# The held-back pair's products with v, moved behind the third bank of scores

## The chip, the cores and the metric

The kernel runs on one core of a Trainium2 chip. The metric is the device time of one execution in microseconds (us), taken over several runs. The core has five engines that run side by side, each through its own queue in order: TensorE (PE, matrix products; its weight loads are listed as PEld), VectorE (DVE), ScalarE (ACT), GpSimd (POOL) and SyncE (SP, which here only issues DMAs). They wait for each other through semaphores.

## The reference

Attention with a sliding window and a distance bias, for 8 batches of 8 heads, 576 positions and 64 channels, followed by a bilinear feed-forward layer on the joined heads:

```
scores = q @ k^T / sqrt(64) - slope[h] * |i - j|     masked to 0 <= i - j < 128
attn   = softmax(scores)          (max subtracted, 1e-9 added to the sum)
x      = attn @ v                 (heads side by side: 4608 tokens x 512)
out    = ((x @ w_a) * (x @ w_b)) @ w_out              (512 -> 1536 -> 512)
```

All inputs and the output are float32. q and k are scaled so that the scores spread over a wide range.

## The kernel before, in words

**Precision.** Nearly all products are done in float16 with each operand split into a high and a low part (high x high, high x low, low x high), accumulated in float32.

**Main work.** After the first batch, which has an order of its own, the program runs `batch(b)` for b = 1 to 7 (the second to the eighth batch). Each does the up products (`up`, 12 blocks of the hidden dimension) and then the down products (`down`). A block of the up products is done in one of two ways: plain (`up_plain`: four groups of twelve 128x128 by 128x288 matmuls, results in a ring of five PSUM banks) or fast (`up_fast`: seven groups of six, with fewer products and more additions). The second batch's blocks are all plain, the third's half and half, the fourth's two plain and ten fast, the later ones' all fast; the plain blocks come first. In the fast way two blocks are under way at once, each as a lane with its own `ch` bank that is written four times; between two writes ACT or DVE has to read it (L932, L944, L955, L967). These reads have a raised priority.

**Side work.** Under the main work of batch b runs the attention of batch b + 1 (`attention`, L710). It handles a batch as four pairs of heads, p = 0 to 3, and each pair in seven steps (the `yield i + k / 7`). For a pair: q and k are loaded, scaled and split (`squares`, `split_qk`, `low_qk`), laid out by SP's DMAs into `qst`, `qkh`, `qkl` (`lay_out_qk`), multiplied into scores in four banks (`scores`, L417: bank 0 holds three tiles, the others two), each followed by a minimum on DVE (L422) and an exponential on ACT (L423) into one of four `t` buffers. `normalize` writes the probabilities, split, into `phl`: the high half on ACT (L439), the low half on DVE (L440). `transpose_probs` (L445) is one transposing DMA from `phl` to `pT`, issued from SP. `pv` multiplies `pT` with the split v (`each_pv`, L541: 42 matmuls of 128x64 weights), and `keep_x` copies the result from PSUM on ACT (L454).

**The held-back pair.** There is one `phl` and one `pT`. Pair 0's probabilities are in `pT` while pair 1's are in `phl`. At p = 1 the products with v are skipped and pair 0 is put into `late`; they are done at p = 2, when v's scale for the batch is known. Only when they are done can pair 1's probabilities go from `phl` into `pT`, and only when that DMA is done may `normalize` of pair 2 write `phl`. `qtot` (L367) is a single small matmul in `split_qk` for the next pair.

**The order.** `Pace` ties the steps of the attention to the groups of the main work: a step is taken when the main work has passed its share. From batch 1 on PE's order is the order of the code (`manual_schedule` for PE). The order on ACT, DVE, POOL and SP is laid out ahead of time by a planner with a model of the run, by readiness and priority, and is then fixed. With `behind()`, an instruction is ordered behind the last main read on its engine. The pair p = 2 of batch b + 1 stands at the start of the up products of batch b: each of its steps takes a fourteenth of `up`, which in the fast way is six groups of six matmuls.

Buffers that matter: the score and product banks `at` are a ring of three (`ps_at`), used at p = 2 in the order scores 0, scores 1, vtot, then the two `x_ps`, qtot, scores 2, scores 3.

Of the kernel before, what the change touches and what calls it, by code (L numbers as in the profile page):

```python
# [46 lines left out]
def attention_then_bilinear_ffn(ctx: ExitStack, tc: tile.TileContext, qT, kT, vP, w_a, w_b, w_out, rel, slopes2, outT):  # L47
# [274 lines left out]
    def new_pT():  # L322
        return work.tile([P, 2 * NCOL // P, P], F16, tag="pT", name="pT")
# [52 lines left out]
    def low_qk(o, behind=None):  # L376
        with tc.issue_after(behind.ins) if behind else ExitStack():
            vec.scalar_tensor_tensor(out=o.kl.rearrange("p h s -> p (h s)"), in0=o.qk.rearrange("p h s -> p (h s)"), scalar=o.own, in1=o.kh.rearrange("p h s -> p (h s)"), op0=ALU.mult, op1=ALU.subtract)
# [23 lines left out]
    def scores(o, bi, ready=None):  # L402

        ps = ps_at.tile([P, 512], F32, tag="at", name="sc_ps")
        t = work.tile([P, 512], F32, tag="t", name="t", bufs=4)
        for i, c in BANKS[bi]:
            w = TILES[i][1]
            qq, kk = slice(64 * i, 64 * i + 64), slice(64 * i + 64 - w, 64 * i + 64)
            if o.b == 1:
                with tc.issue_after(last_pv[0].ins):  # L410
                    for e in range(2):
                        r = slice(64 * e, 64 * e + 64)
                        pe.matmul(ps[r, c:c + w], o.q[r, qq], o.k[r, kk], start=True, stop=True)  # L413
                continue
            for ks, last in ((o.kh, False), (o.kl, True)):
                for e in range(2):
                    pe.matmul(ps[64 * e:64 * e + 64, c:c + w], o.qs[:, e, qq], ks[:, e, kk], start=not last, stop=last)  # L417
        for i, c in BANKS[bi]:
            pc, w = TILES[i]
            n = o.n  # L420
            with tc.issue_after(ready.ins) if ready else ExitStack():
                beside[1] = vec.tensor_tensor_reduce(out=t[:, c:c + w], in0=ps[:, c:c + w], in1=o.bias[:, WIN - w:WIN], scale=-0.125 if o.b == 1 else o.neg, scalar=3.0e38, op0=ALU.add, op1=ALU.min, accum_out=o.mn[:, n:n + 1])  # L422
            beside[0] = act.activation(t[:, c:c + w], t[:, c:c + w], AF.Exp, bias=o.mn[:, n:n + 1], scale=-1.0, accum_out=o.sm[:, n:n + 1])  # L423
            o.parts.append((n, t[:, c:c + w], pc, w))
            o.n += 1
# [17 lines left out]
    def transpose_probs(o):  # L443
        o.pT = new_pT()
        sp.dma_start(o.pT, phl.rearrange("p a c -> p (a c)"), transpose=True)  # L445

    def new_x_ps():
        return [ps_at.tile([P, 512], F32, tag="at", name="x_ps") for _ in range(2)]

    def keep_x(p, st, xp, scale):  # L450

        x = st.v[:, p, 0:S]
        for ps, c, w in ((xp[0], 0, 512), (xp[1], 512, 64)):
            beside[0] = act.activation(x[:, c:c + w], ps[:, 0:w], AF.Copy, scale=scale)  # L454
        square_x(p, st, x)
# [74 lines left out]
    def each_pv(xp, vts, pts):  # L530

        for b in range(5):
            for rows, oc, blocks in by_keys(b):
                w = 64 * len(blocks)
                bank0, o0 = oc < 512, oc % 512
                first = oc == 0 if bank0 else b == 3
                ends = b == 3 if bank0 else b == 4
                for n, (vt, pt) in enumerate(zip(vts, pts)):
                    for h in range(2):
                        c = 512 + 64 * h if b == 4 else 64 * (4 * h + b)  # L540
                        last = pe.matmul(xp[oc // 512][64 * h:64 * h + 64, o0:o0 + w], vt[0:rows, c:c + 64], probs(pt, rows, blocks, h), start=(n == 0 and first), stop=(n == len(vts) - 1 and ends), skip_group_check=True)  # L541
        return last

    def pv(p, st, o, vhl):
        xp = new_x_ps()
        hi, lo = o.pT[:, 0:NCOL // P, :], o.pT[:, NCOL // P:2 * NCOL // P, :]
        each_pv(xp, (vhl[:, 0, :], vhl[:, 1, :], vhl[:, 0, :]), (hi, hi, lo))
        keep_x(p, st, xp, 1.0 / PSC)
# [161 lines left out]
    def attention():  # L710


        n = NPAIR * (B - 1)
        qks = {}

        def load(i):
            if i < n:

                qks[i] = (load_plain_qk if i < NPAIR else load_qk)(1 + i // NPAIR, i % NPAIR)

        def squares(i):
            if i >= n:
                return None
            qk = qks.pop(i)
            return qk if i < NPAIR else qk_squares(1 + i // NPAIR, i % NPAIR, qk)

        def split(o, whole=True):
            if o and o.b > 1:
                split_qk(o)
                if whole:  # L730
                    low_qk(o)

        def lay_out(o):
            if o:
                before_scores(o, lay_out_qk(o) if o.b > 1 else -8.0)

        def behind():

            return tc.issue_after(last_read[0].ins) if last_read[0] else ExitStack()

        load(0)
        st, prev = load_v(1), None
        o = squares(0)
        lay_out(o)
        load(1)
        yield 0
        for i in range(n + 1):
            b, p = 1 + i // NPAIR, i % NPAIR

            two = 2 if o and o.b >= 2 else 1  # L750
            if two == 2 and p == 1:
                with behind():
                    nxt = squares(i + 1)
            for bi in range(two if o else 0):
                scores(o, bi, nxt.ready if two == 2 and p == 1 and nxt else None)
            if two == 1 or p != 1:
                with behind():
                    nxt = squares(i + 1)
            if p == 1 and b > 1:
                st = load_v(b)  # L760
            if p == (1 if b == 1 else 2):
                v_scale(st)
            yield i + 1 / 7
            if o and two == 1:
                scores(o, 1)

            if p == 2:

                with tc.issue_after(first_reads[0].ins) if first_reads[0] else ExitStack():
                    late.vhl = split_v(st, late.p)  # L770
            elif prev and p != 1:
                prev.vhl = split_v(st, prev.p)
            yield i + 2 / 7
            if p == 2:
                pv(late.p, st, late, late.vhl)
                transpose_probs(prev)
                split(nxt)
            if o and p != 2:
                with behind():
                    normalize(o)  # L780
            if p != 2:
                split(nxt, p != 3)
            yield i + 3 / 7
            if o:
                scores(o, 2)
            if p == 3 and nxt and nxt.b > 1:
                low_qk(nxt, beside[1])
            if prev and p not in (1, 2):
                pv(prev.p, st, prev, prev.vhl)
            if two == 2 and p in (1, 3):  # L790
                if p == 2:
                    with behind():
                        normalize(o)
                scores(o, 3)
            yield i + 4 / 7
            if p == 2:
                prev.vhl = split_v(st, prev.p)
                if two == 1 or p not in (1, 3):
                    with behind():
                        normalize(o)  # L800
            if o and (two == 1 or p not in (1, 3)):
                scores(o, 3)
            lay_out(nxt)
            load(i + 2)
            if p == (0 if b == 1 else 1):
                v_squares(st, (0, 1))
            if prev and p == 0:
                states[b - 1] = st
                assert started["down"] == b - 2
                for k, _ in enumerate(split_x(st, b - 1 <= 3, b - 1 >= 2)):  # L810
                    yield i + (4.2 + 0.2 * k) / 7
            yield i + 5 / 7
            if o:
                with behind():
                    normalize(o)
            if p == (0 if b == 1 else 1):
                v_squares(st, (2, 3), vec if b > 2 else act)
            yield i + 6 / 7
            if prev and p == 0:
                hidden_scale(st)  # L820
            if p == 2:
                pv(prev.p, st, prev, prev.vhl)
            if p == 1:
                late = prev
            elif o:
                transpose_probs(o)
            prev, o = o, nxt
            yield i + 1
# [305 lines left out]
```

## Time and profile before

| what | value |
|---|---|
| median of 3 runs | 975.85 us (973.68 to 976.51) |
| the profiled execution | 975.07 us, of which its span 973.3 us |
| TensorE busy | 958.6 us, 98% of the span |
| VectorE, ScalarE busy | 683.1 us, 626.3 us |
| products of probabilities with v in float16 (L541) | 1176 matmuls, 42 for each of 28 pairs |
| transposing DMAs (L445) | 28, 6.9 us from issue to landing (median) |

How to read it: an engine's busy time counts its instructions, not its waits; the matmuls are pipelined, so that a listed length (286 ns for 128x288) is longer than the distance between two starts. In a timeline each line has the start in us from the span's start, the length, the engine, the line of the kernel, the operation, what it writes and reads, and a count where lines are merged; in brackets stands the idle time of that engine just before, with what ended it. "issue" means that nothing that the profile shows was waited for.

### The profile page before, as it was taken

The numbers are of one execution on the slowest core, as the hardware profiler recorded it, in microseconds if no ns is written. First come the engines' busy times: TensorE is split into PE (matmuls) and PEld (weight loads), VectorE is DVE, ScalarE is ACT, GpSimd is POOL, SyncE is SP. The second block draws the span as 40 slices with busy tenths as digits, with TensorE's granted clock in tenths as the row PEclk, the third lists the DMA queues.
The fourth block names the chain that finished last, engine by engine and source line by source line (L and its number), as shares of the span: only waits on it lengthen the run. The fifth ranks groups of instructions, "written<-read, shape, count | busy, mean of one in ns | idle before, by whom it ended". The sixth has DMA issues, their size and how long they took to land.

```text
span 973.3 us, 23844 instructions
## 1 busy us (share of the span) xinstructions
PE 958.6 (98%) x9340; PEld 747.8 (77%) x9341; DVE 683.1 (70%) x1896; ACT 626.3 (64%) x1701; POOL 260.7 (27%) x307
## 2 busy tenths in 40 slices
PE   8989999999999999999999999999999999999998
PEld 6667777777877777777877777777777778877776
DVE  6999998568888768887777877667676676514520
ACT  6878788577776666776766876767666765423321
POOL 1211122044546123631235222401222122301100
PEclk9999999999999999999999999999999999999999
DMA  9463736635347333464246552464245450210001
GB/s 351 143 259 111 254 84 135 146 102 111 90 97 171 75 69 72 109 158 93 52 92 172 101 104 50 111 177 93 45 94 130 117 100 12 57 37 2 1 13 37
DMA packets 148432, 102.82 MB, mean 106 GB/s; under 512 B 120032, under 2 KB 128352, under 8 KB 147296
## 3 DMA queue, kind: packets, MB, share of 16 engines
q1 hardware_dynamic: 138816, 91.77, 38.5%
q10 hardware_dynamic: 9504, 9.54, 3.1%
q8 instruction: 73, 1.20, 0.5%
q14 instruction: 39, 0.32, 0.1%
HBM read 48.33 MB, written 9.44 MB: 59 GB/s over the span
## 4 chain that ended last, share of the span: by engine, by line
PE 86%; DVE 5%; DMA 4%; ACT 3%; issue 1%; SPq 0%; POOL 0%; ACTq 0%; DVEq 0%
PE dn_ps L1003 23%; PE ch L907 19%; PE up_ps L907 17%; PE p L907 15%; PE x_ps L541 5%; PE sc_ps L417 4%; DMA v<-in_vP 2%; PE dn_ps L869 1%; PE sc_ps L413 1%; DMA pT<-phl 1%; DMA wdn<-in_w_b 1%; ACT vsq L309 1%; DVE phl L440 1%; DVE vsq L307 0%; DVE xs L476 0%
## 5 line engine op out<-in xcount | busy, mean ns | idle before, releaser
L907 PEld LDWEIGHTS <-wup 128*128 128x128 f16 x3072 | 296.5, 98 | 84.4 <-issue 7.9
L1003 PE MATMUL dn_ps<-h,wdn 128*128 128x288 f16 x2016 | 253.9, 286 | 0.0
L1003 PEld LDWEIGHTS <-wdn 128*128 128x128 f16 x2016 | 194.0, 98 | 51.8
L907 PE MATMUL up_ps<-xs,wup 128*128 128x288 f16 x1536 | 196.6, 287 | 2.8 <-DVE v L670 2.1
L962 POOL TENSOR_TENSOR rc<-rc,row 128x288 f32<-128x288 f32 x64 | 61.8, 966 | 275.1 <-DVE row L960 259.2
L907 PEld LDWEIGHTS <-wsum 128*128 128x128 f16 x1152 | 111.7, 98 | 30.9 <-issue 1.3
L423 ACT ACTIVATE t<-t,mn 128x192 f32<-128x192 f32 (+2 forms) x252 | 107.2, 427 | 26.4 <-DVE mn L422 26.2
L440 DVE SCALAR_TENSOR_TENSOR phl<-t,rin,phl 128x192 f16<-128x192 f32 (+2 forms) x252 | 107.1, 466 | 15.1 <-ACT phl L439 14.8
L907 PE MATMUL p<-xs,wup 128*128 128x288 f16 x768 | 115.0, 286 | 0.0
L907 PE MATMUL ch<-xs,wup 128*128 128x288 f16 x768 | 115.0, 286 | 0.0
L907 PE MATMUL ch<-xs,wsum 128*128 128x288 f16 x768 | 111.5, 286 | 0.4 <-ACT rc L932 0.4
L439 ACT ACTIVATE phl<-t,rin 128x192 f16<-128x192 f32 (+2 forms) x252 | 88.9, 425 | 29.2 <-DVE rin L436 15.6
L899 ACT CAST h<-rc 128x576 f16<-128x576 f32 x96 | 64.0, 668 | 63.1 <-DVE rc L967 38.1
L900 DVE TENSOR_TENSOR h<-rc,h 128x576 f16<-128x576 f32 x90 | 69.2, 770 | 29.8 <-ACT h L899 29.0
L422 DVE CUSTOM_DVE_ANT_0 t<-sc_ps,bias,neg 128x192 f32<-128x192 f32 (+2 forms) x216 | 73.6, 389 | 10.1 <-PE sc_ps L417 10.0
L1008 ACT ACTIVATE row<-dn_ps,oi 128x288 f32<-128x288 f32 x56 | 27.7, 494 | 57.3 <-PE dn_ps L1003 57.3
L476 DVE TENSOR_TENSOR xs<-v,xs 128x576 f16<-128x576 f32 x52 | 48.0, 934 | 22.5 <-ACT xs L475 22.4
L944 ACT ACTIVATE row<-ch,g 128x288 f32<-128x288 f32 x64 | 31.8, 498 | 49.0 <-PE ch L907 48.9
L398 POOL TENSOR_SCALAR bias<-rel_sb,ninv,sl_sb 128x192 f32<-128x192 f32 x24 | 23.9, 995 | 139.1 <-DVE mn L422 121.1
L939 DVE TENSOR_TENSOR rc<-p,rc 128x288 f32<-128x288 f32 x64 | 29.1, 454 | 44.4 <-PE p L907 34.8
L907 PE MATMUL p<-xs,wsum 128*128 128x288 f16 x384 | 57.5, 286 | 0.0
L967 DVE SCALAR_TENSOR_TENSOR rc<-rc,g,ch 128x288 f32<-128x288 f32 x64 | 32.6, 510 | 23.7 <-PE ch L907 23.6
(158 smaller groups left out, 1381.0 us busy)
## 6 DMA issues: line engine op xcount, KB each, us to landing
v<-in_vP SPq DMA_DIRECT2D x8, 1280.0 KB, 6.2
out<-row ACTq DMA_DIRECT2D x62, 144.0 KB, 1.8
qk<-in_qT SPq DMA_DIRECT2D x28, 288.0 KB, 4.0
qk<-in_kT SPq DMA_DIRECT2D x28, 288.0 KB, 4.4
wdn<-in_w_a SPq DMA_DIRECT2D x12, 512.0 KB, 5.2
wdn<-in_w_b SPq DMA_DIRECT2D x12, 512.0 KB, 6.1
wdn<-in_w_out SPq DMA_DIRECT2D x12, 512.0 KB, 5.0
qst<-qkh SPq DMA_DIRECT2D x24, 144.0 KB, 2.8
```

The source lines that it names most:

```text
L417: pe.matmul(ps[64 * e:64 * e + 64, c:c + w], o.qs[:, e, qq], ks[:, e, kk], start=not last, stop=last)
L422: beside[1] = vec.tensor_tensor_reduce(out=t[:, c:c + w], in0=ps[:, c:c + w], in1=o.bias[:, WIN - w:WIN], scale=-0.125 if o.b == 1 else o. ...
L423: beside[0] = act.activation(t[:, c:c + w], t[:, c:c + w], AF.Exp, bias=o.mn[:, n:n + 1], scale=-1.0, accum_out=o.sm[:, n:n + 1])
L439: beside[0] = last_phl[0] = act.activation(phl[:, 0, pc:pc + w], e, AF.Copy, scale=s)
L440: beside[1] = vec.scalar_tensor_tensor(out=phl[:, 1, pc:pc + w], in0=e, scalar=s, in1=phl[:, 0, pc:pc + w], op0=ALU.mult, op1=ALU.subtract)
L476: vec.tensor_tensor(out=xs[:, n, 1, :, :], in0=src, in1=xs[:, n, 0, :, :], op=ALU.subtract)
L541: last = pe.matmul(xp[oc // 512][64 * h:64 * h + 64, o0:o0 + w], vt[0:rows, c:c + 64], probs(pt, rows, blocks, h), start=(n == 0 and first ...
L899: act.copy(h[:, f, :, 0, :], hid)
L900: eng.tensor_tensor(out=h[:, f, :, 1, :], in0=hid, in1=h[:, f, :, 0, :], op=ALU.subtract)
L907: pe.matmul(ps[:, 0:HT], w[:, wi, k, :], xs[:, b, xi, k, :], start=(first and n == 0), stop=(last and n == len(ks) - 1), skip_group_check= ...
L962: pool.tensor_tensor(out=x0, in0=x0, in1=mid, op=ALU.mult)
L1003: pe.matmul(ps[:, 0:HT], wdn[:, f, wi, e * P:(e + 1) * P], h[:, f, t, hi, :], start=(m == 0 and n == 0), stop=(m == NF - 1 and n == 2))
```

## The change

In `attention`, at p = 2, the products of the held-back pair with v (`pv(late...)`) and the transposing DMA of the pair behind it (`transpose_probs(prev)`) are issued one step later for attentions with `two == 2`, which are those of the third to the eighth batch (b = 2 to 7): behind the matmuls of the third bank of scores (`scores(o, 2)`) and with no main work between the two. `split(nxt)`, with its `qtot` matmul, stays in its place. For the second batch's attention (`two == 1`) nothing changes.

```diff
             yield i + 2 / 7
             if p == 2:
-                pv(late.p, st, late, late.vhl)
-                transpose_probs(prev)
+                if two == 1:
+                    pv(late.p, st, late, late.vhl)
+                    transpose_probs(prev)
                 split(nxt)
             if o and p != 2:
                 with behind():
...
             yield i + 3 / 7
             if o:
                 scores(o, 2)
+            if p == 2 and two == 2:
+                pv(late.p, st, late, late.vhl)
+                transpose_probs(prev)
             if p == 3 and nxt and nxt.b > 1:
                 low_qk(nxt, beside[1])
```

## The prediction

> **What bounds the kernel now.** I read the page first: the engines' busy shares and the chain that ended last.
>
> ```profile
> span 973.3 us, 23844 instructions
> ...
> PE 958.6 (98%) x9340; PEld 747.8 (77%) x9341; DVE 683.1 (70%) x1896; ACT 626.3 (64%) x1701; POOL 260.7 (27%) x307
> ...
> PE 86%; DVE 5%; DMA 4%; ACT 3%; issue 1%; SPq 0%; POOL 0%; ACTq 0%; DVEq 0%
> ```
>
> TensorE is busy for 98% of the span and is 86% of the chain. Next comes the busy time of each engine in two stretches, some 110 us each, late in the program.
>
> ```profile
> 647.00:759.00 112.00, 112.00 (x1120) 87.89 (x1118) 77.84 (x238) 76.18 (x210) 25.62 (x23) 1.00 0.44 103
> 759.00:870.00 111.00, 111.00 (x1068) 87.85 (x1066) 63.11 (x167) 59.69 (x159) 24.43 (x21) 1.00 0.26 57
> ```
>
> The second number of a row is PE's busy time: it fills both stretches at a granted clock of 1.00. There the time is simply the sum of what PE has to do, and anything that shortens PE's work shows one for one, as does anything that makes PE wait. PE's order is written out by hand from the second batch on, so the order that the code gives is the order that runs.
>
> **What the change removes and adds on PE.** It moves 42 matmuls (L541) in each of six attentions, those of the third to the eighth batch. None is added or dropped. What changes is how often PE turns from the 128*128 matmuls of the main work to the 128*64 ones of attention. The timeline of one such place, PE alone (columns: start, length, engine, line):
>
> ```profile
> 660.38 0.90 PE L907 MATMUL ch<-xs,wsum 128*128 128x288 f16 x6
> ...
> 663.32 0.90 PE L907 MATMUL p<-xs,wup 128*128 128x288 f16 x6
> 664.15 1.54 PE L541 MATMUL x_ps<-pT,vhl 128*64 128x128 f16 x42
> 665.62 0.18 PE L367 MATMUL qtot<-both,ones 128*128 128x2 bf16 x1
> 665.66 0.90 PE L907 MATMUL ch<-xs,wup 128*128 128x288 f16 x6
> ...
> 669.41 0.90 PE L907 MATMUL ch<-xs,wup 128*128 128x288 f16 x6
> 670.24 0.27 PE L417 MATMUL sc_ps<-qkh,qst 128*64 128x192 f16 x2
> ...
> 670.51 0.25 PE L417 MATMUL sc_ps<-qkl,qst 128*64 128x192 f16 x2
> 670.69 0.91 PE L907 MATMUL p<-xs,wup 128*128 128x288 f16 x6
> ```
>
> Starts are what counts, because matmuls overlap. From 660.38 to 663.32 there are four groups of six, so one group takes 0.735 us. The visit with v and the single qtot matmul cost 665.66 - 663.32 - 0.735 = 1.605 us. The visit with the third bank of scores costs 670.69 - 669.41 - 0.735 = 0.545 us. Together that is 2.15 us per attention. The trace has the pieces of the new order too, at other places of the same kernel:
>
> ```profile
> 684.87 1.54 PE L541 MATMUL x_ps<-pT,vhl 128*64 128x128 f16 x42
> 686.34 0.91 PE L907 MATMUL p<-xs,wsum 128*128 128x288 f16 x6
> ...
> 699.79 0.90 PE L907 MATMUL p<-xs,wup 128*128 128x288 f16 x6
> 700.52 0.17 PE L367 MATMUL qtot<-both,ones 128*128 128x2 bf16 x1
> 700.55 0.90 PE L907 MATMUL ch<-xs,wup 128*128 128x288 f16 x6
> ...
> 704.37 0.90 PE L907 MATMUL ch<-xs,wup 128*128 128x288 f16 x6
> 705.20 0.27 PE L417 MATMUL sc_ps<-qkh,qst 128*64 128x192 f16 x2
> ...
> 705.55 1.51 PE L541 MATMUL x_ps<-pT,vhl 128*64 128x128 f16 x42
> ```
>
> At 704.37 the fourth pair of the same attention already does what the change does: scores, then products with v, with no gap between (705.20 to 705.55 is the four score steps alone). That gives 705.55 - 704.37 - 0.735 = 0.445 us for the way in and the scores. From the first product with v to the next main matmul are 686.34 - 684.87 = 1.47 us, the way out included. The qtot matmul stays behind alone, and alone it costs 700.55 - 699.79 - 0.735 = 0.025 us. New sum: 0.445 + 1.47 + 0.025 = 1.94 us. One way in and one way out fall away: 2.15 - 1.94 = 0.21 us, and six times that is **1.26 us saved**. Both sides are read from the same rows, so I give this term only 1.0 to 1.5 us, for the 0.01 us in which starts are given (three differences in each sum).
>
> **What the move does off PE.** Behind the products with v stands the transposing DMA of the next pair's probabilities (L445 writes pT, so it waits until the products have read pT). Behind that DMA stand the next pair's normalized probabilities, which overwrite phl (L439 on ACT, L440 on DVE). So this DMA moves with the products, and the rows that follow show how much room it has.
>
> ```profile
> 665.72 4.92 SPq L445 DMA_TRANSPOSE pT<-phl  x1
> 670.81 0.66 SPq L345 DMA_DIRECT2D qk<-in_qT  x1
> ...
> 675.76 0.51 SPq L385 DMA_DIRECT2D qst<-qkh  x1
> ...
> 679.10 0.54 SPq L388 DMA_DIRECT2D qkl<-qkl  x1
> ```
>
> ```profile
> pT<-phl SPq DMA_TRANSPOSE x28, 6.9
> ```
>
> ```profile
> 675.35 2.37 ACT L439 ACTIVATE phl<-t,rin 128x64 f16<-128x64 f32 x7 [0.27 <-DVE rin L436]
> ...
> 679.08 0.37 ACT L932 COPY rc<-ch 128x288 f32<-128x288 f32 x1
> ```
>
> ```profile
> 665.60 0.71 ACT L454 ACTIVATE v<-x_ps 128x512 f32<-128x512 f32 x2 [1.54 <-PE x_ps L541]
> ...
> 666.92 0.68 ACT L460 ACTIVATE xq<-v 128x576 bf16<-128x576 f32 x1
> ...
> 673.84 0.50 ACT L944 ACTIVATE row<-ch,g 128x288 f32<-128x288 f32 x1 [1.32 <-PE ch L907]
> ```
>
> ```profile
> 690.90 0.65 PEld L417 LDWEIGHTS <-qst 128*64 128x64 f16 x20 [0.24 <-issue]
> ```
>
> Now it is issued at 665.72 and lands 6.9 us later, at 672.6, so L439 at 675.35 finds it done with 2.7 us to spare. After the change, all main work between the two places comes 1.6 us earlier: the scores start near 668.7, the products with v end near 670.5, and the DMA goes out near 670.6, 4.9 us later than now. It lands at 677.5. PE's later work stands 0.2 us earlier, so L439 is wanted at 675.15: **the 2.7 us of room become a wait of about 2.3 us**. SP needs 4.92 us to issue the DMA. The loads of L345 and L346 that follow it either go first (0.66 us and a like time for the other: the DMA is then 1.3 us later and the wait 3.6 us), or come after it at 675.5 in place of 670.81; the L385 copies then go out up to 1.3 us later than 675.76. What they feed is done with its last copy issued at 679.10, and the scores that need it run at 690.90, 11.8 us on, which hides 1.3 us. The next products with v (684.87) need the DMA at 684.7, 7 us after it lands. ACT's reads of x_ps (L454) and the square of what they give (L460) move along, 0.71 + 0.68 us; ACT stands idle 1.32 us ahead of L944 at 673.84, and the 1.4 us are free where they stood, so I cost them at nothing; uncovered they would delay one read by 0.1 us.
>
> One sentence group by the Trainium skill, which the rest can do without: "DMA: Bandwidth & Descriptors", section "Latency and other measured facts", gives 261 GB/s for a transposing DMA; the 128 x 4096 two-byte numbers of phl are 1.05 MB, by that page an estimate of 4.0 us. By that figure the DMA would land at 674.6, there would be no wait, and the first rival below would have nothing to stand on. The row above says 6.9 us for this transfer, and I use the row.
>
> What does the wait cost? L439 stands in ACT's queue, L440 behind it in DVE's, and the queue behind them holds main reads. The main work at this place:
>
> ```profile
> 678.61 1.79 PE L907 MATMUL ch<-xs,wsum 128*128 128x288 f16 x12
> 680.23 0.90 PE L907 MATMUL p<-xs,wsum 128*128 128x288 f16 x6
> ```
>
> Two groups of six take 680.23 - 678.61 = 1.62 us there and not 1.47: the second group rewrites the bank that L932 reads from 679.08 to 679.45, and waits 0.15 us for it. L932 comes that late because it stands behind the seven L439. So there is no slack at that point now. If the ACT order stayed as it is, all 2.3 us would reach PE. But the order on ACT and DVE isn't written by hand: a planner lays it out from its own times, puts a ready main read ahead (its priority is raised), and knows of the DMA. It will probably put main reads before L439 that now come behind it. The cost per attention therefore lies between -0.15 us (L932 goes ahead and the present wait goes) and +2.3 us (+3.6 with the loads first). It applies in four of the six attentions; in the other two the main work has plain groups of twelve matmuls in a ring of five banks, where a bank comes round again only after four more groups, 4 x 1.47 = 5.9 us, which hides 3.6 us. I take 0, near the lower end: L932's lateness stays as it is, since it's the row at this very place. The bounds for four are -0.6 to +9.2 us, or +14.4.
>
> **Sum.** The profiled execution took 975.07 us, 1.77 us beyond its span, and the median of the runs shown is 975.85 us (973.68 to 976.51). 975.07 - 1.26 + 0 = 973.8 us for an execution like the profiled one; on the median of the runs 975.85 - 1.26 = **974.6 us**. The gain is 0.13%, less than the 0.3% (2.9 us) that a measurement of this kernel can tell from no change.
>
> **Rivals.** First, slower: L439 and L440 hold their queues, and main reads behind them come late. There is a place in this trace where ACT's queue does wait for this DMA:
>
> ```profile
> ACT phl L439 <- DMA pT<-phl: 11.8, 7, 2.9
> ```
>
> ```profile
> 746.70 5.46 SPq L445 DMA_TRANSPOSE pT<-phl  x1
> ...
> 752.43 0.16 DVE L371 CUSTOM_DVE_ANT_0 own<-sc,halves 128x2 f32<-128x2 f32 x1
> ...
> 754.55 1.68 ACT L439 ACTIVATE phl<-t,rin 128x64 f16<-128x64 f32 x5 [2.89 <-DMA pT<-phl]
> ...
> 756.13 1.24 ACT L373 ACTIVATE qkh<-qk,own 128x1152 f16<-128x1152 f32 x1
> ```
>
> L373 had its scale at 752.6 and started at 756.13: the planned order doesn't step round a DMA that is later than the plan has it. PE lost nothing there, but that is in the down products, where an output is read only once in some 3.7 us. Under the fast up products such a wait falls on a bank with no room. If half of the 2.3 us reach PE in four attentions, that is 4.6 - 1.26 = +3.3 us, 979.2 us; with all of it 9.2 - 1.26 = +7.9 us, 983.8 us. It decides the sign from 0.32 us per attention on (1.26 / 4), and passes 0.3% from 1.05 us on. Against it: raised priorities, and that the plan holds the DMA's own wait. Chance 0.24.
>
> Second, a larger gain: with L439 planned later, L932 goes ahead of it and the four waits of 0.15 us vanish as well: -1.26 - 0.6 = -1.9 us, 974.0 us. For it speaks that the wait is on record; against it, that L440 then presses on DVE's reads in turn. Chance 0.12.
>
> Third, the change doesn't save: the way out of the longer visit costs what the two did, or a new order on ACT or DVE takes 0.2 us per attention elsewhere. Then the time stays at 975.85 us. Against it stand the rows at 705.20 and 705.55, where the two meet without a gap. Chance 0.12. The forecast itself keeps 0.52.
>
> **How the numbers follow.** The runs shown scatter from 2.2 us below to 0.7 us above their median, so a median of a few moves by about 1 us. The forecast with that is 973.4 to 975.8; the lower end takes in the second rival, 973.0, and the upper end reaches half-way into the first, to 980.0. Left out is the rest of the first rival and a little below. Faster by over 0.3% needs under 972.9: only the second rival with favourable scatter, and the edge of the forecast, 0.10. Slower by over 0.3% is above 978.8: most of the first rival, 0.19. The rest, 0.71, is no change that can be told.
>
> **What would show it.** Right: in six places the L541 group starts straight after the L417 group of the third bank, one pair of ways in and out is missing, and from group to group the combined visit costs 1.9 us. The L445 issue stands 4.9 us later against the main work. Wrong for the cost: PE rows waiting for L932, L944, L950, L955 or L939 just after, and an L439 row waiting for the DMA pT<-phl in the third pair's place. The forecast fails if those waits sum to over 1 us per attention, or if PE's busy stretch there no longer equals the stretch.

## The result, and the profile after

| | before | after |
|---|---|---|
| median of 5 runs | 975.4 us | 999.05 us (996.18 to 1000.1) |
| span of the profiled execution | 973.3 us | 997.8 us |

The ratio is 1.0232, with a 95% interval of 1.0219 to 1.0245: the change made the kernel 2.3% slower. Line numbers below L785 have moved by four in the changed kernel: L907 is now L911, L932 is L936, L955 is L959, L1003 is L1007.

The page of the changed kernel: span, busy shares, and the chain that ended last, by engine and by line.

```profile
span 997.8 us, 23835 instructions
...
PE 968.4 (97%) x9340; PEld 753.3 (75%) x9341; DVE 682.9 (68%) x1896; ACT 625.9 (63%) x1701; POOL 260.1 (26%) x307
...
PE 83%; DMA 6%; ACT 4%; DVE 4%; issue 1%; POOL 1%; ACTq 0%; DVEq 0%; POOLq 0%
PE dn_ps L1007 22%; PE ch L911 17%; PE up_ps L911 17%; PE p L911 13%; DMA pT<-phl 5%; PE x_ps L541 4%; PE sc_ps L417 3%; PE dn_ps L873 3%; PE sc_ps L413 1%; ACT t L423 1%; ACT phl L439 1%; DMA v<-in_vP 1%; DVE phl L440 1%; PE warm_ps L69 0%; PE sc_ps L612 0%
```

PE's work is the same, but it takes 9.8 us more and is no longer the whole span, and the transposing DMA pT<-phl now holds 5% of the chain (0.7% before). PE's three longest waits (who, on whom, us in total, times, the longest), and the two late stretches:

```profile
PE ch L911 <- DVE rc L959: 6.2, 3, 2.4
PE ch L911 <- ACT rc L936: 5.4, 5, 1.8
PE ch L911 <- DVE rc L971: 3.4, 1, 3.4
```

```profile
647.00:759.00 112.00, 108.24 (x1080) 84.79 (x1078) 76.60 (x235) 73.35 (x203) 22.75 (x21) 0.98 0.43 99
759.00:870.00 111.00, 107.07 (x1036) 83.53 (x1035) 66.88 (x194) 63.54 (x175) 20.23 (x20) 0.97 0.37 79
```

Where before PE filled these stretches at a clock of 1.00, it now waits some 4 us in each, and the clock has come down. To place the loss I measured one stretch in each attention: from the first `vtot` matmul of the third pair to the first score of the fourth. The moved work lies in between. For the attention of the seventh batch (b = 6), kernel before, then after:

```profile
655.13 0.25 PE L318 MATMUL vtot<-vc,ones 128*128 128x1 bf16 x4
...
690.90 0.22 PE L417 MATMUL sc_ps<-qkh,qst 128*64 128x64 f16 x2
```

```profile
668.07 0.25 PE L318 MATMUL vtot<-vc,ones 128*128 128x1 bf16 x4
...
708.83 0.22 PE L417 MATMUL sc_ps<-qkh,qst 128*64 128x64 f16 x2
```

That is 35.77 us before and 40.76 us after. The same difference of the same two starts for all six attentions and all kernels, in us (the runs are told below):

| kernel | b=2 | b=3 | b=4 | b=5 | b=6 | b=7 |
|---|---|---|---|---|---|---|
| before | 30.94 | 45.99 | 38.67 | 35.78 | 35.77 | 35.77 |
| after | 30.73 | 46.95 | 45.18 | 41.67 | 40.76 | 42.38 |
| e1_dma_late | 30.95 | 45.98 | 38.67 | 35.77 | 35.77 | 35.77 |
| e2_norm_late | 30.72 | 46.44 | 43.62 | 35.17 | 35.18 | 35.17 |
| e3_no_dma_new | 30.72 | 45.75 | 38.85 | 35.47 | 35.46 | 36.21 |
| e4_no_dma_old | 30.95 | 45.99 | 38.66 | 35.79 | 35.77 | 35.77 |
| e5_dma_held | 30.95 | 47.61 | 43.61 | 40.44 | 40.85 | 40.48 |
| e6_last_three | 30.95 | 45.98 | 38.66 | 35.17 | 35.17 | 35.21 |
| e7_loads_behind | 30.72 | 46.41 | 41.52 | 37.57 | 40.54 | 40.67 |
| e8_norm_late_alone | 30.95 | 45.98 | 38.66 | 35.58 | 35.48 | 35.49 |
| e9_fill | 30.72 | 46.52 | 44.34 | 39.08 | 41.42 | 37.93 |
| e10_four | 30.73 | 45.98 | 38.66 | 35.17 | 35.17 | 35.25 |

The differences of the first two rows sum to -0.21 + 0.96 + 6.51 + 5.89 + 4.99 + 6.61 = 24.8 us; the spans differ by 24.5 us. So the whole loss lies in these stretches, nearly all of it in the four under the fast up products. In b = 2, under plain products, the change brings just the 0.21 us that the visits were to save.

One loss step by step, b = 6 of the changed kernel. PE's combined visit:

```profile
681.53 0.27 PE L417 MATMUL sc_ps<-qkh,qst 128*64 128x192 f16 x2
...
681.89 1.51 PE L541 MATMUL x_ps<-pT,vhl 128*64 128x128 f16 x42
683.33 0.91 PE L911 MATMUL p<-xs,wup 128*128 128x288 f16 x6
```

The two parts meet without a gap, as forecast. SP's queue then:

```profile
682.54 0.65 SPq L345 DMA_DIRECT2D qk<-in_qT  x1
683.24 0.61 SPq L346 DMA_DIRECT2D qk<-in_kT  x1
683.90 6.04 SPq L445 DMA_TRANSPOSE pT<-phl  x1
```

The loads go first, and the transposing DMA goes out at 683.90. ACT:

```profile
691.92 0.98 ACT L439 ACTIVATE phl<-t,rin 128x64 f16<-128x64 f32 x3 [4.20 <-DMA pT<-phl]
...
693.37 1.49 ACT L439 ACTIVATE phl<-t,rin 128x192 f16<-128x192 f32 x4
...
695.64 0.37 ACT L936 COPY rc<-ch 128x288 f32<-128x288 f32 x1
```

L439 waits 4.20 us for the DMA, which takes 8.0 us from issue to this start. L936, a main read, still stands behind all seven L439: it starts 3.72 us after the first of them (691.92 to 695.64), as L932 did before the change (675.35 to 679.08, 3.73 us). And PE:

```profile
690.51 0.90 PE L911 MATMUL p<-xs,wup 128*128 128x288 f16 x6
693.37 0.90 PE L911 MATMUL ch<-xs,wsum 128*128 128x288 f16 x6 [1.96 <-DVE rc L959]
696.07 1.60 PE L911 MATMUL ch<-xs,wsum 128*128 128x288 f16 x6 [1.81 <-ACT rc L936]
697.46 1.65 PE L911 MATMUL p<-xs,wsum 128*128 128x288 f16 x6
698.90 1.04 PE L911 MATMUL ch<-xs,wup 128*128 128x288 f16 x6
699.77 0.90 PE L911 MATMUL p<-xs,wup 128*128 128x288 f16 x6
```

PE waits twice. By the starts, the two groups from 690.51 to 696.07 take 5.56 us in place of 2 x 0.735 = 1.47 us: 4.09 us lost (the bracketed 1.96 and 1.81 us count from the listed end of the last matmul, which lies behind the time at which the next could have started). After that the three groups from 696.07 to 699.77 take 3.70 us in place of 2.21 us. The granted clock is the number behind POOL's count in the stretches that follow:

```profile
694.00:696.00 2.00, 0.26 (x3) 0.08 (x1) 2.00 (x5) 2.00 (x8) 1.17 (x1) 0.94 0.50 114
696.00:698.00 2.00, 1.93 (x9) 1.23 (x9) 1.57 (x5) 0.92 (x3) 0.00 (x0) 0.50 0.00 0
698.00:700.00 2.00, 2.00 (x13) 1.41 (x12) 0.71 (x3) 1.16 (x5) 0.00 (x0) 0.71 0.00 0
```

It halves after the idle time and costs another 1.49 us. 4.09 + 1.49 = 5.58 us. From that go the 0.21 us saved and the 0.15 us for which PE waited for L932 here before. Two more short waits of the kernel before are gone too:

```profile
667.12 1.71 PE L907 MATMUL ch<-xs,wsum 128*128 128x288 f16 x12
668.67 0.90 PE L907 MATMUL p<-xs,wsum 128*128 128x288 f16 x6
...
681.11 0.90 PE L907 MATMUL ch<-xs,wup 128*128 128x288 f16 x6
```

The two groups from 667.12 took 1.55 us and not 1.47 us, and the group from 680.23 to 681.11 took 0.88 us and not 0.735 us. 5.58 - 0.21 - 0.15 - 0.08 - 0.15 = 4.99 us, as in the table.

### The profile page after: what moved, and what is told of

It is laid out like the page before. It is cut to its first block, busy times and chain, and to the rows that moved or that the text cites. A ratio compares the mean times of both kernels' runs of the same rounds, so it can differ in the third digit from the quotient of the medians.

```text
span 997.8 us, 23835 instructions
## 1 busy us (share of the span) xinstructions
PE 968.4 (97%) x9340; PEld 753.3 (75%) x9341; DVE 682.9 (68%) x1896; ACT 625.9 (63%) x1701; POOL 260.1 (26%) x307
## 4 chain that ended last, share of the span: by engine, by line
PE 83%; DMA 6%; ACT 4%; DVE 4%; issue 1%; POOL 1%; ACTq 0%; DVEq 0%; POOLq 0%
PE dn_ps L1007 22%; PE ch L911 17%; PE up_ps L911 17%; PE p L911 13%; DMA pT<-phl 5%; PE x_ps L541 4%; PE sc_ps L417 3%; PE dn_ps L873 3%; PE sc_ps L413 1%; ACT t L423 1%; ACT phl L439 1%; DMA v<-in_vP 1%; DVE phl L440 1%; PE warm_ps L69 0%; PE sc_ps L612 0%
## 5 line engine op out<-in xcount | busy, mean ns | idle before, releaser
L911 PEld LDWEIGHTS <-wup 128*128 128x128 f16 x3072 | 298.9, 99 | 91.3 <-issue 11.9
L1007 PE MATMUL dn_ps<-h,wdn 128*128 128x288 f16 x2016 | 253.9, 286 | 0.0
L1007 PEld LDWEIGHTS <-wdn 128*128 128x128 f16 x2016 | 193.9, 98 | 51.8
L911 PE MATMUL up_ps<-xs,wup 128*128 128x288 f16 x1536 | 196.3, 287 | 2.0 <-DVE v L670 1.8
L911 PEld LDWEIGHTS <-wsum 128*128 128x128 f16 x1152 | 113.6, 99 | 44.8 <-issue 13.2
L440 DVE SCALAR_TENSOR_TENSOR phl<-t,rin,phl 128x192 f16<-128x192 f32 (+2 forms) x252 | 108.9, 473 | 37.4 <-ACT phl L439 37.2
L911 PE MATMUL ch<-xs,wsum 128*128 128x288 f16 x768 | 114.1, 291 | 11.6 <-DVE rc L959 6.2
L911 PE MATMUL ch<-xs,wup 128*128 128x288 f16 x768 | 118.0, 291 | 4.5 <-DVE rc L971 3.4
L439 ACT ACTIVATE phl<-t,rin 128x192 f16<-128x192 f32 (+2 forms) x252 | 89.1, 425 | 49.0 <-DMA pT<-phl 35.7
L911 PE MATMUL p<-xs,wup 128*128 128x288 f16 x768 | 117.2, 290 | 0.2 <-ACT rc L954 0.2
L948 ACT ACTIVATE row<-ch,g 128x288 f32<-128x288 f32 x64 | 31.8, 496 | 46.2 <-PE ch L911 46.0
L911 PE MATMUL p<-xs,wsum 128*128 128x288 f16 x384 | 59.8, 294 | 0.0
```

Source lines behind the costliest of these rows:

```text
L439: beside[0] = last_phl[0] = act.activation(phl[:, 0, pc:pc + w], e, AF.Copy, scale=s)
L440: beside[1] = vec.scalar_tensor_tensor(out=phl[:, 1, pc:pc + w], in0=e, scalar=s, in1=phl[:, 0, pc:pc + w], op0=ALU.mult, op1=ALU.subtract)
L911: pe.matmul(ps[:, 0:HT], w[:, wi, k, :], xs[:, b, xi, k, :], start=(first and n == 0), stop=(last and n == len(ks) - 1), skip_group_check= ...
L1007: pe.matmul(ps[:, 0:HT], wdn[:, f, wi, e * P:(e + 1) * P], h[:, f, t, hi, :], start=(m == 0 and n == 0), stop=(m == NF - 1 and n == 2))
```

## The experiments

**The DMA issued from a later line of the program.** In e1_dma_late the products stay, and only the call that issues the DMA moves.

```diff
             if p == 2:
                 pv(late.p, st, late, late.vhl)
-                transpose_probs(prev)
+                if two == 1:
+                    transpose_probs(prev)
                 split(nxt)
...
                 scores(o, 2)
+            if p == 2 and two == 2:
+                transpose_probs(prev)
```

> The products of the held-back pair stay at their old place, as before; only the transposing DMA behind them is issued late, behind the third bank of scores, where the changed kernel has it. Theory (the DMA lands late, L439 holds ACT's queue, main reads come late and TensorE's clock then halves): as slow as the changed kernel or a little slower, 995 to 1003 us, with L439 waiting some 4 us for pT<-phl in the third pairs and PE waiting for L936 and L959. Rival (the longer visit of TensorE itself, or its PSUM banks, hurts): the visit is gone, so 975 to 977 us.

Measured: 975.58 us, ratio 1.0002 (0.9991 to 1.0013). By my expectation that would have felled the theory. But the trace shows that the DMA was not late at all:

```profile
662.63 1.54 PE L541 MATMUL x_ps<-pT,vhl 128*64 128x128 f16 x42
```

```profile
664.20 4.92 SPq L445 DMA_TRANSPOSE pT<-phl  x1
```

It goes out 1.57 us after the products start, exactly as before (665.72 - 664.15). SP's order isn't written by hand, and the planner issues the DMA as soon as pT has been read. So this run tells nothing of a late DMA; what it shows is that in the change it was the move of the products, not the move of the call, that made the DMA late.

**The DMA held back by data.** e5_dma_held makes it really late, with the visits as before: a tiny copy from the third bank of scores into pT, which the DMA then overwrites.

```diff
             o.n += 1
+        return ps
...
-    def transpose_probs(o):
+    def transpose_probs(o, third=None):
         o.pT = new_pT()
+        if third is not None:
+            vec.tensor_copy(o.pT[:, 0, 0:1], third[:, 0:1])
         sp.dma_start(o.pT, phl.rearrange("p a c -> p (a c)"), transpose=True)
...
                 pv(late.p, st, late, late.vhl)
-                transpose_probs(prev)
+                if two == 1:
+                    transpose_probs(prev)
...
-                scores(o, 2)
+                third = scores(o, 2)
+            if p == 2 and two == 2:
+                transpose_probs(prev, third)
```

> The kernel before, products with v at their old place; between them and the transposing DMA of the second pair stands a copy of 128 x 1 numbers on DVE from the third bank of scores into pT, which the DMA must wait for (third to eighth batch). So the DMA leaves PE's visits as they were and goes out at about the place where the changed kernel has it (some 1 us earlier against the scores), 5 to 6 us later than before. Theory (the late DMA is the cause): L439 waits 2 to 4 us for pT<-phl in the third pairs, PE waits behind it, 985 to 1000 us. Rival (the longer visit is the cause): 975 to 977 us.

Measured: 996.12 us, ratio 1.0206 (1.0188 to 1.0223). Its SP, ACT and PE in b = 6 (L439 is L440 here, L932 is L938):

```profile
682.91 5.76 SPq L448 DMA_TRANSPOSE pT<-phl  x1
```

```profile
691.06 2.36 ACT L440 ACTIVATE phl<-t,rin 128x64 f16<-128x64 f32 x7 [3.03 <-DMA pT<-phl]
693.33 0.38 ACT L938 COPY rc<-ch 128x288 f32<-128x288 f32 x1
```

```profile
693.75 1.60 PE L913 MATMUL ch<-xs,wsum 128*128 128x288 f16 x6 [3.70 <-ACT rc L938]
695.15 1.64 PE L913 MATMUL p<-xs,wsum 128*128 128x288 f16 x6
```

The DMA goes out 8.2 us after the products start (674.70) and not 1.57 us. PE's visits are those of the kernel before, and yet four attentions lose 4.7 to 5.1 us each. The copy itself is 0.16 us on DVE for each attention. So a late DMA is enough by itself; the longer visit isn't needed for the loss.

**The visit without the DMA.** The other half: the products moved, but the transposing DMA of the second pair left out in b = 2 to 7 (that pair then uses the first pair's probabilities). e4_no_dma_old leaves it out with the products at the old place. The edit of e3_no_dma_new, against the changed kernel:

```diff
                 pv(late.p, st, late, late.vhl)
-                transpose_probs(prev)
+                prev.pT = late.pT
```

> The changed kernel without the transposing DMA of the second pair in the attentions of the third to the eighth batch: that pair's products then use the first pair's probabilities, so part of the work is left out. Theory: no wait and no slow clock are left, and the saving of the visit shows alone: PE in those parts about 0.2 us per attention shorter than in the same kernel with the products at the old place (next run), 973 to 975 us. Rival (the longer visit hurts): above 985 us.

> The kernel before with the same DMA left out: the partner of the run above. Both theories: like the kernel before, 974.5 to 976 us, since that DMA keeps nobody waiting there.

Measured: 974.72 us (ratio 0.9994, 0.9983 to 1.0005) and 975.62 us (1.0002, 0.9992 to 1.0012). In the table the move is worth 0.23, 0.24, 0.32 and 0.31 us in b = 2, 3, 5 and 6. In b = 4 it loses 0.19 and in b = 7 it loses 0.44 us: in b = 7 PE waits 0.47 us for L948 10 us ahead of the moved products, so it is a shift of the planned order that costs there. In b = 4 the trace of e3_no_dma_new has ACT reading x_ps (L454) and working on it (L329, L460) right ahead of the main read L954, and PE waits for L954 at 450.32, 0.41 us by the starts: there the reads that move along with the products cost more than the visit saves. The total of this pair of runs does not tell a gain from none; the stretches do.

**Normalizing later.** If what hurts is the queue behind the waiting L439, it is enough to plan L439 later. In e2_norm_late the first three banks of the third pair are normalized one step later, together with the fourth, in b = 5 to 7 of the changed kernel.

```diff
             if p == 2:
                 prev.vhl = split_v(st, prev.p)
-                if two == 1 or p not in (1, 3):
+                if not (b >= 5):
                     with behind():
                         normalize(o)
```

> The changed kernel, with the third pair's probabilities of banks 0 to 2 normalized one step later, together with bank 3, in the last three attentions (b = 5 to 7). Nothing else moves. Theory (what stands behind the waiting L439 is what hurts): the feed-forward parts of the fifth, sixth and seventh batch lose their waits, each again about 0.2 us shorter than before the change; those three cost 5.7 + 5.0 + 6.6 = 17.3 us in the changed kernel, so 981 to 983 us. Rival (the longer visit hurts): 996 to 1000 us.

Measured: 979.55 us, ratio 1.0041 (1.0028 to 1.0053). The three attentions fall from 41.67, 40.76 and 42.38 us to 35.17 or 35.18, 0.60 us under the kernel before, with the products still in their new place: the 0.21 us of the visit and the three short waits of before, 0.38 us. ACT in b = 6 of this run:

```profile
687.13 0.40 ACT L936 COPY rc<-ch 128x288 f32<-128x288 f32 x1
687.42 3.06 ACT L439 ACTIVATE phl<-t,rin 128x64 f16<-128x64 f32 x9
```

L439 comes after the main read and finds the DMA done. What is left, 4.1 us over the 975.48 us of the kernel before in the same runs, is mostly b = 4 (43.62 for 38.67 us), where the edit doesn't reach.

**The same two edits apart, and as a version.** e8_norm_late_alone has this edit in the kernel before; e6_last_three has both edits in b = 5 to 7 alone; e10_four adds the move in b = 2. The edit of e10_four, against the kernel before:

```diff
-                pv(late.p, st, late, late.vhl)
-                transpose_probs(prev)
+                if b not in (2, 5, 6, 7):
+                    pv(late.p, st, late, late.vhl)
+                    transpose_probs(prev)
...
                 scores(o, 2)
+            if p == 2 and b in (2, 5, 6, 7):
+                pv(late.p, st, late, late.vhl)
+                transpose_probs(prev)
...
-                if two == 1 or p not in (1, 3):
+                if not (b >= 5):
                     with behind():
                         normalize(o)
```

> The kernel before, products at their old place, with the normalizing of the first three banks one step later in the last three attentions (b = 5 to 7). Theory: this alone takes away the 0.15 us for which PE waits for L932 in each, and the move the other part of the 0.60 us, so 0.15 to 0.39 us shorter in each; 974.4 to 975.4 us. Rival: the whole 0.6 us is the normalizing's, and the visit saves nothing.

> The products moved behind the third bank in the last three attentions alone (b = 5 to 7), and there the normalizing of the first three banks one step later too; everything else as before. In the run with the late normalizing these three came out 0.60 us shorter each than before the change, from 655.13 to 690.90 = 35.77 us to 35.17 us. Theory: that adds up, 3 x 0.6 = 1.8 us less than before, 973 to 975 us, and PE waits nowhere in them. Rival (the gain there came from a shift of the whole order): 975 to 977 us.

> Products moved in the attentions b = 2, 5, 6 and 7, normalizing late in the last three; as before in b = 3 and 4. Theory: the attention of the third batch is 0.21 us shorter (30.94 to 30.73 us in the changed kernel), the last three 0.60 us each: 2.0 us less than before, a ratio of 0.998, 973 to 974.5 us. Rival (the move gains nothing): ratio 0.999 to 1.000, from the late normalizing alone.

Measured: 974.78 us (ratio 0.9991, 0.9981 to 1.0), 974.27 us (0.9988, 0.9978 to 0.9997) and 974.07 us (0.9983, 0.9974 to 0.9992). In the stretches the late normalizing alone is worth 0.20 to 0.29 us (the two waits of 0.15 us), and the move on top of it 0.28 to 0.41 us (the visit's 0.21 us and the 0.08 us at 667.12, mostly). The wait of PE for L932 that the prediction found before is gone with it; in e6_last_three two groups take 679.90 - 678.43 = 1.47 us there:

```profile
678.43 1.63 PE L911 MATMUL ch<-xs,wsum 128*128 128x288 f16 x12
679.90 0.90 PE L911 MATMUL p<-xs,wsum 128*128 128x288 f16 x6
```

So the visit's saving is real, and e10_four with its 0.17% is a little faster than both kernels. Its interval just clears 1; the gain is below the 0.3% that the prediction took as telling.

**How the loss follows the DMA's time.** e7_loads_behind orders the loads of q and k behind the transposing DMA.

```diff
-        sp.dma_start(o.pT, phl.rearrange("p a c -> p (a c)"), transpose=True)
+        o.tr = sp.dma_start(o.pT, phl.rearrange("p a c -> p (a c)"), transpose=True)
...
-            load(i + 2)
+            with tc.issue_after(prev.tr.ins) if p == 2 and two == 2 else ExitStack():
+                load(i + 2)
```

> The changed kernel, with the loads of q and k (L345, L346) ordered on SP behind the transposing DMA in the third pairs. In the changed kernel they go first there: the DMA goes out some 0.4 us late for that and lands after 8.0 us instead of 6.9. Theory (each us that the DMA is late costs a us of PE and more): L439 waits 2 to 3 us instead of 4.2, 985 to 994 us. Rival (the longer visit): unchanged, 997 to 1000 us.

Measured: 992.76 us, ratio 1.0176 (1.0159 to 1.0193). In two of the attentions, b = 5 and b = 6, SP and ACT:

```profile
562.78 4.74 SPq L445 DMA_TRANSPOSE pT<-phl  x1
```

```profile
569.59 0.99 ACT L439 ACTIVATE phl<-t,rin 128x64 f16<-128x64 f32 x3 [2.51 <-DMA pT<-phl]
```

```profile
676.08 5.51 SPq L445 DMA_TRANSPOSE pT<-phl  x1
```

```profile
684.24 0.98 ACT L439 ACTIVATE phl<-t,rin 128x64 f16<-128x64 f32 x3 [3.87 <-DMA pT<-phl]
```

In b = 5 the DMA lands in 6.8 us, L439 waits 2.51 us and the stretch loses 37.57 - 35.78 = 1.8 us. In b = 6 it takes 8.2 us although the loads are behind it, the wait is 3.87 us and the loss 4.8 us. So loads ahead of it are not the only thing that makes this DMA slow; what else does I don't know. The step from 1.8 to 4.8 us for 1.36 us more of wait is too steep for the wait alone. By the starts PE waits 0.43 and 1.97 us in b = 5, where its clock stays at 1.00, and 1.78 and 1.98 us in b = 6, where the groups that follow take 1.62 us more than at full clock: 1.36 + 1.62 = 3.0 us. The granted clock (the number behind POOL's) in b = 4, with one PE wait of 2.5 us, and in b = 6, with 1.6 + 1.8 us:

```profile
440.00:470.00 30.00, 27.05 (x287) 21.21 (x285) 19.53 (x51) 17.81 (x46) 3.87 (x5) 1.00 0.42 80
```

```profile
670.00:700.00 30.00, 26.57 (x270) 20.36 (x269) 19.28 (x50) 17.06 (x44) 5.35 (x6) 0.94 0.47 90
```

**The clock by itself.** e9_fill gives PE something to do where it would wait first: 36 more matmuls into unused columns of a bank of scores, in b = 5 to 7 of the changed kernel.

```diff
             o.n += 1
+        return ps
...
-                scores(o, 3)
+                fourth = scores(o, 3)
...
+            if p == 2 and b >= 5:
+                yield i + 4.75 / 7
+                for _ in range(36):
+                    pe.matmul(fourth[:, 192:320], ones16, ones16, start=True, stop=True)
             yield i + 5 / 7
```

> The changed kernel with 36 matmuls of 128 columns more on PE in the last three attentions (b = 5 to 7), some 2 us, at the place where PE waits first for L959; they write unused columns of a bank of scores, so they add work and no result. They keep TensorE busy where it would wait. Theory (a part of the loss is the clock, which halves after the idle time): the waits for the DMA stay, but the granted clock stays at 1.00 in those three attentions, so each is 1 to 3 us shorter than in the changed kernel (41.67, 40.76 and 42.38 us from vtot to the fourth pair's scores); 992 to 997 us. Rival (the slow matmuls are no matter of idle time): 999 us or, with the added work, up to 1005 us.

Measured: 993.07 us, ratio 1.0167 (1.0152 to 1.0183). b = 5 is the clean one. First the changed kernel, then this run, each with its clock over the same 24 us:

```profile
579.17 1.60 PE L911 MATMUL ch<-xs,wsum 128*128 128x288 f16 x6 [1.10 <-ACT rc L936]
...
583.29 0.90 PE L911 MATMUL p<-xs,wup 128*128 128x288 f16 x6
```

```profile
568.00:592.00 24.00, 20.45 (x177) 14.87 (x176) 13.60 (x33) 12.59 (x33) 5.02 (x6) 0.86 0.56 107
```

```profile
579.58 0.90 PE L916 MATMUL ch<-xs,wsum 128*128 128x288 f16 x6 [1.74 <-ACT rc L941]
...
581.78 0.90 PE L916 MATMUL p<-xs,wup 128*128 128x288 f16 x6
```

```profile
568.00:592.00 24.00, 22.26 (x247) 17.72 (x245) 15.31 (x40) 14.93 (x41) 5.84 (x6) 1.00 0.65 131
```

Three groups take 583.29 - 579.17 = 4.12 us at the halved clock and 581.78 - 579.58 = 2.20 us with the fill: 1.9 us for the clock alone, while the second wait for ACT is still there. b = 5 and b = 7 come out 2.6 and 4.4 us shorter than in the changed kernel, with a clock of 1.00. b = 6 is 0.7 us longer: its clock fell in spite of the fill, after waits of 0.44 and 1.81 us. The planner also laid out a new order here, so the differences of the whole stretches are not the clock's alone; the three groups are.

## Why the prediction was wrong

- **What bounds the kernel: right.** PE's busy time filled the stretches, and every us that PE waited showed in the total.
- **The visits, 0.21 us each: right.** b = 2 gained 0.21 us, and without the DMA four of six attentions gained 0.23 to 0.32 us. What was not right is the cost of nothing for the reads of x_ps that move along: in b = 4 PE waits 0.41 us behind them.
- **The DMA's lateness: the mechanism right, the size too small.** The prediction had L439 waiting 2.3 us, or 3.6 us with the loads first. In b = 6 it waited 4.20 us. The loads did go first, but held the DMA back by 0.44 us only (it goes out 683.90 - 681.89 = 2.01 us after the products start, and 1.57 us before the change); then it took 8.0 us and not the median of 6.9 us. The median was the wrong row for this place: the trace of the kernel before has the DMA issued at 665.72 landing after 8.5 us (6.7 to 6.9 us in b = 4, 5 and 7), so L439 had 1.1 us of room there and not 2.7 us.
- **The step that failed** is the cost of that wait: "It will probably put main reads before L439 that now come behind it", and with that the value of 0 taken from bounds of -0.15 to +2.3 (+3.6) us. ACT's order at this place stayed, L936 behind all seven L439, and of the 4.20 us on ACT nearly all reached PE, 4.09 us in b = 6. The prediction had read the two facts that make this likely, that L932 had no slack there and that the planned order didn't step round a late DMA at 754.55, and gave them to a rival with a chance of 0.24. e2_norm_late shows that step to be the cause in b = 5 to 7: with L439 planned later, the loss is gone with everything else in place.
- **The upper bound was too low as well**, because it priced waiting alone. By the starts, with 0.735 us for a group, waiting took 3.6, 4.6, 4.1 and 4.0 us in b = 4 to 7 of the changed kernel, 16.2 us, and the groups at the slow clock after it 2.7, 1.9, 1.5 and 2.8 us more, 8.9 us. Less 0.84 us for four visits and 1.1 us of short waits that are gone (0.38 us in each of b = 5 to 7), with new short waits of 0.39 us for L954 in b = 4 and 0.46 us for L948 in b = 7, that is 24.0 us, as in the table for these four. The first rival, priced at 4 x 2.3 - 1.26 = +7.9 us, was thus the right case at a third of its size.
- **The second rival was priced low.** Late normalizing takes away two waits of 0.15 us in an attention, not one; but only b = 5 to 7 have them.
- **Plain products hide 3.6 us: not quite.** b = 3 lost 0.96 us. Its plain groups lose nothing, but the first fast groups behind them wait 0.75 us for L924 and 0.47 us for L936 (0.18 us before the change). Whether late normalizing helps there too wasn't tried.

## What to carry to other kernels

When work is moved later, price what its result releases, not only the work: here 42 matmuls moved by 5 us and pushed a DMA past the place where two in-order queues need it. If a row shows a read with no slack behind the instruction that will wait, the wait should be charged in full until an order that avoids it is shown. And under the fast up products here the merged visit paid only once the consumer of the moved release was moved by a step too.

## What the runs showed of the hardware

TensorE's granted clock fell to 0.50 after idle times of some us, and the price was about half of the waiting, 8.9 us on 16.2 us. It stayed at 1.00 after a single wait of 2.50 us (b = 4 of e7_loads_behind) and after waits of 0.27 + 1.81 us with one group of six between (b = 5 of the same run). It fell after single waits of 3.45 us (b = 4 of the changed kernel), 3.70, 3.10 and 2.85 us (b = 6, 4 and 5 of e5_dma_held), and after two waits with one group of six between, 1.96 + 1.81 us (b = 6 of the changed kernel) and 0.44 + 1.81 us (b = 6 of e9_fill). So 2.25 us in two parts lowered it and 2.50 us in one did not: the length alone doesn't decide, and what else does is not shown here. The shortest of the single waits that lowered it:

```profile
577.03 1.25 PE L913 MATMUL ch<-xs,wsum 128*128 128x288 f16 x6 [2.85 <-ACT rc L938]
578.07 1.65 PE L913 MATMUL p<-xs,wsum 128*128 128x288 f16 x6
```

The clock was 0.93 from 577.0 to 577.5 and 0.50 from 577.5 on. By the starts this wait is 3.02 us long. The slow time was 2 to 4 groups, some 3 to 6 us. The Trainium skill, "TensorE: Matmul & The Clock Gate", section "What's actually happening", has the array fall to half clock after an idle window of about 3.4 us that runs freely. The waits of 2.50, 3.45 and 3.70 us fit that. The falls after 2.85 and 3.10 us (0.17 us more by the starts), and after two waits with work between, each under 2 us, don't: less than one unbroken idle window was enough, and here the measurement decides.

The transposing DMA of the same 1.05 MB took 6.8 and 8.2 us in two attentions of one kernel (e7_loads_behind, b = 5 and b = 6), from its issue to the start that waited for it. SP was busy 4.74 and 5.51 us of that with issuing it.
